# Weight sums moved into the room of the conversion's buffers (three and six of them), the first weight piece converted ahead of the fourth chunk's scores, and the conversion steps dealt out anew

## The chip, the cores and the metric

One core of a Trainium2 chip. The metric is the device time of one execution in microseconds (us); a profile's span is about 2 us shorter. The granted TensorE clock is given where it matters. Names of engines: PE is TensorE's matmul, PEld its weight load, DVE is VectorE, ACT ScalarE, POOL GpSimd, SPq the queue that issues DMAs.

## The reference, cut to what matters

```python
# q, k, v: (8, 8, 576, 64) float32; w1, w2, w3: (512, 768), w_out: (768, 512), all float64
scores = q @ k.T / 8;  ret = scores * decay_mask;  attn = ret @ v       # per batch and head
x = attn.transpose(0, 2, 1, 3).reshape(4608, 512)
h = maximum(maximum(x @ w1, x @ w2), x @ w3)
return (h @ w_out).astype(float32)
```

The weights arrive as float64. The kernel reads them as pairs of 32-bit words and builds float32 values: 24 pieces of 128x512, each by four VectorE steps, three ScalarE steps and one product on GpSimd.

## The kernel before

Attention runs in 36 chunks of 128 tokens, the maxout layer in 9 tiles of 512 tokens. Tile 0 uses plain matrix products and takes place while the weights are being converted; the later tiles use a Strassen-like scheme with sums of weights, which must wait for converted ones. Conversion is a generator; `convert(n)` runs n of its steps, and these calls are strewn between the products, so they fix the order of instructions on VectorE, ScalarE and GpSimd.

```python
wraw = ...tile_pool(name="wraw", bufs=WAHEAD)      # WAHEAD = 4: raw 64-bit pieces
wtmp = ...tile_pool(name="wtmp", bufs=2)           # expo and mant of a piece
...
def convert_all():
    last = None
    for piece in pieces + [None]:
        if piece:                                                       # step a
            nc.vector.tensor_scalar(out=expo[:], in0=high, scalar1=0x7FF00000, ...)        # "mask"
            nc.scalar.activation(mant[:], low, ...)
        yield
        if piece:                                                       # step b
            nc.scalar.activation(expo...)
            nc.vector.tensor_scalar(out=frac[:], in0=high, scalar1=0xFFFFF, ...)
        yield
        if last:                                                        # step c, of the piece before
            nc.vector.scalar_tensor_tensor(out=e[:], in0=h, ..., in1=e[:], ...)            # "sign"
            nc.gpsimd.tensor_tensor(w, m[:], e[:].bitcast(FP32), op=ALU.mult)              # "product"
            load_weights(1)
        if piece: nc.scalar.activation(expo...)
        yield
        if piece:                                                       # step d
            nc.vector.scalar_tensor_tensor(out=mant[:], in0=frac[:], ..., in1=mant[:], ...)# "whole"
        yield
        last = piece and (piece, high, expo, mant)
...
def ffn(t):                                       # tile 0
    for n, (fp, i) in enumerate(units):           # 3 groups fp, 3 weights i
        for fb in (2 * fp, 2 * fp + 1):
            up_plain(t, h, fb, i)                 # 4 matmuls; i == 0: ScalarE copies h,
            convert(7 if i == 0 else 4)           # i > 0: VectorE takes the maximum
        yield                                     # (a step of attention's next chunk comes here)
    convert(4 * len(pieces) + 4)
    ... down(t, h, m) ...                         # 4 x 6 matmuls with w_out
...
    scores(2); scores(3)
    convert(2)
    values(2)
    convert(3); decay_values(4)
    values(3)
    convert(3)
```

Each matmul written here is two instructions of 4-byte data in the trace, so a piece's product of 4 matmuls is 8 instructions.

Of the kernel before, what the change touches and what calls it, by code (L numbers as in the profile page):

```python
# [46 lines left out]
AHEAD = 3  # L47
WAHEAD = 4


@with_exitstack
def kernel(
# [37 lines left out]
    wraw = while_converting.enter_context(tc.tile_pool(name="wraw", bufs=WAHEAD))  # L90
    wtmp = while_converting.enter_context(tc.tile_pool(name="wtmp", bufs=2))
    ps_r = ctx.enter_context(tc.tile_pool(name="ps_r", bufs=4, space=PSUM))
# [175 lines left out]
    def sums_of_outs():  # L268

        while_converting.close()  # L270
        pool = ctx.enter_context(tc.tile_pool(name="late", bufs=1))
        lo, hi = slice(0, DM // 2), slice(DM // 2, DM)
# [84 lines left out]
    def convert_all():  # L357


        last = None  # L360
        for piece in pieces + [None]:
            if piece:
                raw_bits = bits.pop(piece)
                words = raw_bits[:].bitcast(I32).rearrange("p (f two) -> p f two", two=2)
                high = words[:, :, 1]
                low = raw_bits[:].bitcast(U32).rearrange("p (f two) -> p f two", two=2)[:, :, 0]
                expo = wtmp.tile([P, DM], I32, tag="expo", name="expo")
                mant = wtmp.tile([P, DM], FP32, tag="mant", name="mant")
                nc.vector.tensor_scalar(out=expo[:], in0=high, scalar1=0x7FF00000, scalar2=None, op0=ALU.bitwise_and)  # L369
                nc.scalar.activation(mant[:], low, AF.Identity, bias=one[:], scale=2.0 ** -52)  # L370
            yield
            if piece:
                nc.scalar.activation(expo[:].bitcast(FP32), expo[:], AF.Relu, bias=top[:], scale=-8.0)
                frac = wtmp.tile([P, DM], I32, tag="frac", name="frac", bufs=1)
                nc.vector.tensor_scalar(out=frac[:], in0=high, scalar1=0xFFFFF, scalar2=None, op0=ALU.bitwise_and)
            yield
            if last:
                (i, fb), h, e, m = last
                nc.vector.scalar_tensor_tensor(out=e[:], in0=h, scalar=-2 ** 31, in1=e[:],  # L379
                                               op0=ALU.bitwise_and, op1=ALU.bitwise_or)  # L380
                if i == "out":
                    w = w_sb[i, fb] = w_out[:, fb // 2, fb % 2, :]
                else:
                    w = w_sb[i, fb] = const.tile([P, DM], FP32, name=f"w{i}_{fb}")[:]
                nc.gpsimd.tensor_tensor(w, m[:], e[:].bitcast(FP32), op=ALU.mult)  # L385
                load_weights(1)
            if piece:
                nc.scalar.activation(expo[:], expo[:].bitcast(FP32), AF.Relu, bias=inf[:], scale=-1.0)
            yield
            if piece:  # L390
                nc.vector.scalar_tensor_tensor(out=mant[:], in0=frac[:], scalar=2.0 ** -20, in1=mant[:],
                                               op0=ALU.mult, op1=ALU.add)
            yield
            last = piece and (piece, high, expo, mant)

    def weight_sums(n):
        if n >= len(units):
            return
        fp, i = units[n]
        half = [slice(0, DM // 2), slice(DM // 2, DM)]  # L400
        b11, b21 = (w_sb[i, 2 * fp][:, r] for r in half)
        b12, b22 = (w_sb[i, 2 * fp + 1][:, r] for r in half)
        t1, t2, t4 = (const.tile([P, DM // 2], FP32, name=f"T{m}_{i}_{fp}")[:] for m in (1, 2, 4))
        nc.vector.tensor_tensor(t1, b12, b11, op=ALU.subtract)
        nc.vector.tensor_tensor(t2, b22, t1, op=ALU.subtract)
        nc.gpsimd.tensor_tensor(b12, b22, b12, op=ALU.subtract)
        nc.gpsimd.tensor_tensor(t4, b21, t2, op=ALU.subtract)
        wT[fp, i] = {1: b11, 2: b21, 3: b22, 4: t4, 5: t1, 6: t2, 7: b12}
# [3 lines left out]
    def convert(n):  # L412
        for _ in range(n):
            next(converting, None)
# [56 lines left out]
    def down(t, h, m):  # L471
        ps = ps_y.tile([P, DM], FP32, tag="y", name="down")
        for fb in range(NF):
            nc.tensor.matmul(ps[:], lhsT=h[:, fb, m * P:(m + 1) * P], rhs=w_sb["out", fb],  # L474
                             start=(fb == 0), stop=(fb == NF - 1))
        osb = wtmp.tile([P, DM], FP32, tag="mant", name="osb")
        nc.scalar.copy(osb[:], ps[:])
# [12 lines left out]
    def ffn(t):  # L490

        h = hpool.tile([P, NF, NT], FP32, tag="h", name="h")
        for n, (fp, i) in enumerate(units):
            if t == 0:
                for fb in (2 * fp, 2 * fp + 1):
                    up_plain(t, h, fb, i)
                    convert(7 if i == 0 else 4)
            else:
# [9 lines left out]
        if t == 0:  # L508
            convert(4 * len(pieces) + 4)
            for m in range(NT // P):  # L510
# [21 lines left out]
    load(4)  # L532
    load_weights(2)
    decay_values(0)
# [11 lines left out]
    values(1)  # L546
    scores(2)
    scores(3)
    convert(2)
    values(2)  # L550
    convert(3)
    decay_values(4)
    values(3)
    convert(3)
    for t in range(N // NT):
        work = ffn(t)
        for g in range((t + 1) * CPT, (t + 2) * CPT):
            for step in (transposes, scores, values):
                if g < NG:
                    if step is transposes and g + 1 < NG:  # L560
                        load(g + 1)
                    if step is scores and g + 1 < NG:
                        decay_values(g + 1)
                    step(g)
                next(work, None)
# [51 lines left out]
```

## Time and profile before

| what | before |
|---|---|
| median time of the first runs | 848.0 us |
| span of the profile | 845.1 us |
| PE busy | 830.1 us, 98% |
| start of the first up product | 33.40 us |
| start of the first down product | 114.33 us |
| first product of the second tile | 144.76 us |

The table by stretches, cut at these three places, has in each line the stretch, its length, the busy time of each engine with its count of instructions (in the order PE, PEld, DVE, ACT, POOL), the granted clock of TensorE (1.00 is full), the DMA share and GB/s. It is the view to begin with.

```profile
0.00:33.40 33.40, 27.24 (x252) 24.07 (x252) 14.84 (x27) 11.05 (x17) 12.45 (x19) 1.00 0.80 199
33.40:114.30 80.90, 80.34 (x312) 40.93 (x313) 57.01 (x105) 48.75 (x73) 38.16 (x25) 0.98 0.55 161
114.30:144.80 30.50, 27.15 (x99) 13.27 (x98) 15.10 (x21) 5.17 (x9) 13.25 (x11) 0.94 0.22 55
144.80:845.10 700.30, 695.40 (x3977) 594.32 (x3975) 327.46 (x652) 110.07 (x297) 125.93 (x127) 1.00 0.26 54
```

The last stretch has five sixths of the time, and TensorE is busy in all but 5 us of it. What can be won lies in the first three: idle time, and a clock of 0.98 and 0.94, which "busy" does not show.

### The profile page before, as it was taken

The page shows a single profiled execution, that of the slowest core. Times are in us where ns is not written, and L with a number is a line of the kernel's source. Part 1 is how long each engine was busy: PE and PEld are TensorE (multiplying, and loading weights), DVE is VectorE, ACT ScalarE, POOL GpSimd, SP SyncE. Part 2 cuts the span into 40 slices and gives each one's busy share as a digit, 9 for nine tenths or more (in the row PEclk, how much of TensorE's full clock was granted, in tenths as well). Part 3 has the DMA queues.
Part 4 walks back from the last instruction along what each step waited for, and adds up shares of the span by engine and source line. Part 5 has one row for each costly group of instructions (what it writes and reads, how often), then busy time and mean ns, then how long its engine had stood idle before and what let it go on. Part 6 is the DMA issues. An engine that isn't in the chain of part 4 may idle for free.

```text
span 845.1 us, 12652 instructions
## 1 busy us (share of the span) xinstructions
PE 830.1 (98%) x4636; PEld 672.6 (80%) x4636; DVE 414.4 (49%) x803; ACT 175.0 (21%) x395; POOL 189.8 (22%) x182
## 2 busy tenths in 40 slices
PE   9799989999999999999999999999999999999998
PEld 8455445878888888888888888888888888888887
DVE  2577754575445534554454435444345435433341
ACT  3356731111011111111111111111111111111211
POOL 3345544254301211111111121112011202201000
PEclk9999999999999999999999999999999999999999
DMA  9636631333223322333133323332333224201001
GB/s 233 166 125 187 187 69 58 56 56 56 57 53 75 57 55 54 56 62 82 50 56 54 57 77 56 56 56 68 69 54 55 50 62 77 50 14 37 1 1 50
DMA packets 232509, 59.06 MB, mean 70 GB/s; under 512 B 213504, under 2 KB 230912, under 8 KB 232448
## 3 DMA queue, kind: packets, MB, share of 16 engines
q1 hardware_dynamic: 232304, 58.26, 30.7%
q8 instruction: 36, 0.59, 0.3%
q14 instruction: 25, 0.20, 0.1%
q10 hardware_dynamic: 144, 0.00, 0.0%
HBM read 48.76 MB, written 9.44 MB: 69 GB/s over the span
## 4 chain that ended last, share of the span: by engine, by line
PE 86%; DVE 6%; POOL 4%; issue 1%; SPq 1%; DMA 0%; ACT 0%; DVEq 0%; POOLq 0%
PE x L425 28%; PE z L425 14%; PE dx L312 10%; PE y L425 7%; PE dz L312 5%; PE s L183 4%; PE o L213 4%; PE kv L194 4%; PE o L218 4%; POOL w L385 3%; PE dy L312 2%; PE down L474 2%; DVE expo L379 2%; DVE expo L369 1%; SPq L146 1%
## 5 line engine op out<-in xcount | busy, mean ns | idle before, releaser
L425 PE MATMUL x<-S,T 128*128 128x256 f32 x576 | 147.8, 379 | 0.0
L425 PEld LDWEIGHTS x<-S,T 128*128 128x128 f32 x576 | 109.2, 190 | 15.2
L156 POOL TENSOR_TENSOR vd<-vraw,gk 128x512 f32<-128x512 f32 x36 | 38.3, 1064 | 340.6 <-DMA vraw<-in_v_dram 334.5
L425 PE MATMUL x<-S,w 128*128 128x256 f32 x288 | 74.6, 381 | 1.4 <-DVE h L455 1.4
L425 PE MATMUL x<-xT,w 128*128 128x256 f32 x288 | 74.8, 382 | 0.0
L425 PE MATMUL z<-S,w 128*128 128x256 f32 x288 | 73.9, 379 | 0.0
L425 PE MATMUL z<-xT,T 128*128 128x256 f32 x288 | 73.9, 379 | 0.0
L425 PE MATMUL y<-xT,w 128*128 128x256 f32 x288 | 73.9, 379 | 0.0
L430 ACT COPY p<-x 128x256 f32<-128x256 f32 x72 | 26.8, 372 | 220.6 <-PE x L425 217.9
L455 DVE TENSOR_TENSOR tmp<-x,p 128x256 f32<-128x256 f32 x48 | 20.4, 425 | 102.4 <-PE x L425 102.4
L483 PE MATMUL up<-xT,w 128*128 128x512 f32 x144 | 65.8, 609 | 4.8 <-POOL w L385 4.7
L186 DVE TENSOR_TENSOR st<-s,causal 128x512 f32<-128x512 f32 x72 | 46.4, 685 | 48.3 <-PE s L183 48.3
L425 PEld LDWEIGHTS x<-S,w 128*128 128x128 f32 x288 | 49.3, 189 | 15.2 <-DVE h L455 2.4
L425 PEld LDWEIGHTS z<-S,w 128*128 128x128 f32 x288 | 54.7, 190 | 7.4
L425 PEld LDWEIGHTS y<-xT,w 128*128 128x128 f32 x288 | 54.7, 190 | 7.4
L425 PEld LDWEIGHTS z<-xT,T 128*128 128x128 f32 x288 | 54.0, 189 | 8.2
L220 DVE TENSOR_TENSOR xT<-o,gq 128x512 f32<-128x512 f32 x36 | 24.8, 690 | 72.2 <-PE o L218 66.2
L425 PEld LDWEIGHTS x<-xT,w 128*128 128x128 f32 x288 | 51.5, 190 | 6.6 <-issue 0.8
L483 PEld LDWEIGHTS up<-xT,w 128*128 128x128 f32 x144 | 27.0, 194 | 37.3 <-issue 29.8
L295 POOL TENSOR_TENSOR H<-h 128x256 f32<-128x256 f32 x24 | 18.6, 774 | 150.4 <-DVE h L468 150.4
L430 ACT COPY u<-x 128x256 f32<-128x256 f32 x72 | 26.8, 372 | 99.9 <-PE x L425 99.9
L183 PEld LDWEIGHTS s<-qT,kT 64*128 64x128 f32 x576 | 35.7, 191 | 13.6 <-issue 11.1
(92 smaller groups left out, 1203.6 us busy)
## 6 DMA issues: line engine op xcount, KB each, us to landing
bits<-in_moe_w_dram SPq DMA_DIRECT2D x18, 512.0 KB, 3.6
out_dram<-osb SPq DMA_DIRECT2D x36, 256.0 KB, 2.1
kraw<-in_k_dram SPq DMA_DIRECT2D x32, 256.0 KB, 3.0
vraw<-in_v_dram SPq DMA_DIRECT2D x32, 256.0 KB, 3.5
qraw<-in_q_dram SPq DMA_DIRECT2D x448, 16.0 KB, 1.8
kxraw<-in_k_dram SPq DMA_DIRECT2D x448, 16.0 KB, 1.8
bits<-in_moe_w_out_dram SPq DMA_DIRECT2D x6, 512.0 KB, 3.5
qraw<-in_q_dram SPq DMA_DIRECT2D x7, 256.0 KB, 4.4
```

Of the source, the lines that this page charges most:

```text
L156: nc.gpsimd.tensor_tensor(t[:], raws.pop(("v", g))[:], gk[:].unsqueeze(2).to_broadcast([C, H, D]), op=ALU.mult)
L183: nc.tensor.matmul(s[j][:, p, :], lhsT=kT[r, p, :], rhs=qT[r, p, :], start=True, stop=True)
L186: nc.vector.tensor_tensor(st[:, j], s[j][:], masks[start_of(g)][:].unsqueeze(1).to_broadcast([C, NP, C]), op=ALU.mult)
L194: nc.tensor.matmul(kv[:, p, :], lhsT=pair(kr, p)[r:], rhs=pair(vds[g], p)[r:], start=True, stop=True)
L213: nc.tensor.matmul(o[D * j:D * (j + 1), p, :], lhsT=vr[:, 2 * p + j, :], rhs=st[:, j, p, :], start=(p == 0), stop=(old == 0 and p == NP - ...
L218: nc.tensor.matmul(o[:, p, :old], lhsT=sd[:, p, :], rhs=qT[:, p, :old], start=False, stop=(p == NP - 1), skip_group_check=True)
L220: nc.vector.tensor_tensor(xT[t][:, :, i * C:(i + 1) * C], o[:], gq[:], op=ALU.mult)
L312: nc.tensor.matmul(out[:, m, :], lhsT=hS[n](fp)[:, m * P:(m + 1) * P], rhs=late["T"][n][:, fp, :], start=first and m == 0 and fp == 0, sto ...
L385: nc.gpsimd.tensor_tensor(w, m[:], e[:].bitcast(FP32), op=ALU.mult)
L425: nc.tensor.matmul(out[:], lhsT=w[:, d * P:(d + 1) * P], rhs=xS[t][n][:, d, :], start=first and d == 0, stop=d == 1, skip_group_check=True)
L430: nc.scalar.copy(c[:], src[:])
L483: nc.tensor.matmul(ps[:], lhsT=w_sb[i, fb][:, dc * P:(dc + 1) * P], rhs=xT[t][:, dc, :], start=(dc == 0), stop=(dc == NDC - 1))
```

## The change

The intent: conversion should be ahead of TensorE. The sums of weights, 27 tiles of 1 KB per partition, leave the constants for a pool that opens when conversion's buffers are closed; that pays for a third pair of expo and mant and two more raw buffers. The first piece is masked before the fourth chunk's scores and multiplied right after them. The numbers of steps are dealt out anew.

```diff
-WAHEAD = 4
+WAHEAD = 6
-    wtmp = while_converting.enter_context(tc.tile_pool(name="wtmp", bufs=2))
+    wtmp = while_converting.enter_context(tc.tile_pool(name="wtmp", bufs=3))
... (sums: const.tile -> late["pool"].tile; the outputs' osb: wtmp -> opool; load_weights(2) -> (4) before attention)
+        for n, piece in enumerate(pieces):
+            high, expo, mant, frac = yield from masks(bits.pop(piece))   # steps a, b
+            if last:
+                product(*last)                                          # step c
+                yield
+            whole(mant, frac)                                           # step d
             yield
+            last = piece, high, expo, mant
+            if n == 0:
+                product(*last)
+                yield
+                last = None
+        product(*last)
+        yield
...
-                    convert(7 if i == 0 else 4)
+                    convert(4 if i > 0 else 8 if fp == 1 else 6)
...
     scores(2)
+    convert(3)
+    values(2)
+    decay_values(4)
     scores(3)
+    convert(1)
+    transposes(4)
     convert(2)
-    values(2)
-    convert(3)
-    decay_values(4)
     values(3)
-    convert(3)
+    convert(4)
```

More of the change, by code (lines that the diff above doesn't have):

```diff
@@ L268, in sums_of_outs @@
     def sums_of_outs():
-        while_converting.close()
-        pool = ctx.enter_context(tc.tile_pool(name="late", bufs=1))
+        pool = late["pool"]
         lo, hi = slice(0, DM // 2), slice(DM // 2, DM)
@@ L357, in convert_all @@
     def convert_all():
-        last = None
-        for piece in pieces + [None]:
-            if piece:
-                raw_bits = bits.pop(piece)
-                words = raw_bits[:].bitcast(I32).rearrange("p (f two) -> p f two", two=2)
-                high = words[:, :, 1]
-                low = raw_bits[:].bitcast(U32).rearrange("p (f two) -> p f two", two=2)[:, :, 0]
-                expo = wtmp.tile([P, DM], I32, tag="expo", name="expo")
-                mant = wtmp.tile([P, DM], FP32, tag="mant", name="mant")
-                nc.vector.tensor_scalar(out=expo[:], in0=high, scalar1=0x7FF00000, scalar2=None, op0=ALU.bitwise_and)
-                nc.scalar.activation(mant[:], low, AF.Identity, bias=one[:], scale=2.0 ** -52)
-            yield
-            if piece:
-                nc.scalar.activation(expo[:].bitcast(FP32), expo[:], AF.Relu, bias=top[:], scale=-8.0)
-                frac = wtmp.tile([P, DM], I32, tag="frac", name="frac", bufs=1)
-                nc.vector.tensor_scalar(out=frac[:], in0=high, scalar1=0xFFFFF, scalar2=None, op0=ALU.bitwise_and)
-            yield
-            if last:
-                (i, fb), h, e, m = last
-                nc.vector.scalar_tensor_tensor(out=e[:], in0=h, scalar=-2 ** 31, in1=e[:],
-                                               op0=ALU.bitwise_and, op1=ALU.bitwise_or)
-                if i == "out":
-                    w = w_sb[i, fb] = w_out[:, fb // 2, fb % 2, :]
-                else:
-                    w = w_sb[i, fb] = const.tile([P, DM], FP32, name=f"w{i}_{fb}")[:]
-                nc.gpsimd.tensor_tensor(w, m[:], e[:].bitcast(FP32), op=ALU.mult)
-                load_weights(1)
-            if piece:
-                nc.scalar.activation(expo[:], expo[:].bitcast(FP32), AF.Relu, bias=inf[:], scale=-1.0)
-            yield
-            if piece:
-                nc.vector.scalar_tensor_tensor(out=mant[:], in0=frac[:], scalar=2.0 ** -20, in1=mant[:],
-                                               op0=ALU.mult, op1=ALU.add)
-            yield
-            last = piece and (piece, high, expo, mant)
@@ new lines, in masks @@
+        def masks(raw_bits):
+            words = raw_bits[:].bitcast(I32).rearrange("p (f two) -> p f two", two=2)
+            high = words[:, :, 1]
+            low = raw_bits[:].bitcast(U32).rearrange("p (f two) -> p f two", two=2)[:, :, 0]
+            expo = wtmp.tile([P, DM], I32, tag="expo", name="expo")
+            mant = wtmp.tile([P, DM], FP32, tag="mant", name="mant")
+            nc.vector.tensor_scalar(out=expo[:], in0=high, scalar1=0x7FF00000, scalar2=None, op0=ALU.bitwise_and)
+            nc.scalar.activation(mant[:], low, AF.Identity, bias=one[:], scale=2.0 ** -52)
+            yield
+            nc.scalar.activation(expo[:].bitcast(FP32), expo[:], AF.Relu, bias=top[:], scale=-8.0)
+            frac = wtmp.tile([P, DM], I32, tag="frac", name="frac", bufs=1)
+            nc.vector.tensor_scalar(out=frac[:], in0=high, scalar1=0xFFFFF, scalar2=None, op0=ALU.bitwise_and)
+            nc.scalar.activation(expo[:], expo[:].bitcast(FP32), AF.Relu, bias=inf[:], scale=-1.0)
+            yield
+            return high, expo, mant, frac
@@ new lines, in whole, with product @@
+        def whole(mant, frac):
+            nc.vector.scalar_tensor_tensor(out=mant[:], in0=frac[:], scalar=2.0 ** -20, in1=mant[:],
+                                           op0=ALU.mult, op1=ALU.add)
+        def product(piece, high, expo, mant):
+            i, fb = piece
+            nc.vector.scalar_tensor_tensor(out=expo[:], in0=high, scalar=-2 ** 31, in1=expo[:],
+                                           op0=ALU.bitwise_and, op1=ALU.bitwise_or)
+            if i == "out":
+                w = w_sb[piece] = w_out[:, fb // 2, fb % 2, :]
+            else:
+                w = w_sb[piece] = const.tile([P, DM], FP32, name=f"w{i}_{fb}")[:]
+            nc.gpsimd.tensor_tensor(w, mant[:], expo[:].bitcast(FP32), op=ALU.mult)
+            load_weights(1)
@@ L396, in weight_sums @@
+        last = None
+        for n, piece in enumerate(pieces):
[4 more added lines that the diff above has]
+            whole(mant, frac)
+            yield
+            last = piece, high, expo, mant
+            if n == 0:
+                product(*last)
+                yield
+                last = None
+        product(*last)
+        yield
     def weight_sums(n):
@@ L402, in weight_sums @@
         b12, b22 = (w_sb[i, 2 * fp + 1][:, r] for r in half)
-        t1, t2, t4 = (const.tile([P, DM // 2], FP32, name=f"T{m}_{i}_{fp}")[:] for m in (1, 2, 4))
+        t1, t2, t4 = (late["pool"].tile([P, DM // 2], FP32, name=f"T{m}_{i}_{fp}")[:] for m in (1, 2, 4))
         nc.vector.tensor_tensor(t1, b12, b11, op=ALU.subtract)
@@ L475, in down @@
                              start=(fb == 0), stop=(fb == NF - 1))
-        osb = wtmp.tile([P, DM], FP32, tag="mant", name="osb")
+        osb = opool.tile([P, DM], FP32, tag="osb", name="osb")
         nc.scalar.copy(osb[:], ps[:])
@@ L508, in ffn @@
         if t == 0:
-            convert(4 * len(pieces) + 4)
+            convert(4 * len(pieces))
+            while_converting.close()
+            late["pool"] = ctx.enter_context(tc.tile_pool(name="late", bufs=1))
             for m in range(NT // P):
@@ L532 @@
     load(4)
-    load_weights(2)
+    load_weights(4)
     decay_values(0)
@@ L563 @@
                         decay_values(g + 1)
-                    step(g)
+                    if g > CPT or step is not transposes:
+                        step(g)
                 next(work, None)
```

## The prediction

> **What bounds the kernel now.** I read the page first. TensorE leads it, and nothing else is near.
>
> ```profile
> PE 830.1 (98%) x4636; PEld 672.6 (80%) x4636; DVE 414.4 (49%) x803; ACT 175.0 (21%) x395; POOL 189.8 (22%) x182
> ```
>
> 98% of 845.1 us leaves 15.0 us without a matmul, so a change that only moves work can win little more than that. The table by stretches says where it lies: from 200 to 835 us TensorE is busy without a gap (sum 0), and the last 11 us hold 4.4 us of landing output. About 10.6 us are left, all before 200 us. Next the view of waits for TensorE alone:
>
> ```profile
> PE up L483 <- POOL w L385: 4.7, 1, 4.7
> PE down L474 <- POOL w_out L385: 3.4, 2, 2.6
> PE warm L113 <- POOL ident masks.py:199: 1.4, 1, 1.4
> PE x L425 <- DVE h L455: 1.4, 2, 0.7
> PE o L213 <- DVE st L186: 0.4, 2, 0.2
> ```
>
> Two waits carry it, both for converted weights (GpSimd's multiplication ends a piece): one before the first piece of all, one before the last pieces of w_out. Then the timeline of the weight loads, which shows the pitch of the matmuls (the matmul rows merge and their ends are modelled):
>
> ```profile
> 33.40 0.30 PEld L483 LDWEIGHTS up<-xT,w 128*128 128x128 f32 x2 [4.89 <-POOL w L385]
> 34.00 0.33 PEld L483 LDWEIGHTS up<-xT,w 128*128 128x128 f32 x1 [0.30 <-issue]
> 34.86 0.33 PEld L483 LDWEIGHTS up<-xT,w 128*128 128x128 f32 x1 [0.52 <-issue]
> 35.71 0.33 PEld L483 LDWEIGHTS up<-xT,w 128*128 128x128 f32 x1 [0.52 <-issue]
> 36.56 0.33 PEld L483 LDWEIGHTS up<-xT,w 128*128 128x128 f32 x1 [0.52 <-issue]
> 37.35 0.19 PEld L483 LDWEIGHTS up<-xT,w 128*128 128x128 f32 x1 [0.46 <-issue]
> 37.78 0.19 PEld L483 LDWEIGHTS up<-xT,w 128*128 128x128 f32 x1 [0.24 <-issue]
> ...
> 120.54 0.30 PEld L474 LDWEIGHTS down<-w_out,h 128*128 128x128 f32 x2 [3.42 <-POOL w_out L385]
> 122.43 0.37 PEld L474 LDWEIGHTS down<-w_out,h 128*128 128x128 f32 x2 [1.59 <-POOL w_out L385]
> 124.30 1.77 PEld L183 LDWEIGHTS s<-qT,kT 64*128 64x128 f32 x16 [1.50 <-issue]
> ```
>
> The reader is to see that a wait costs more than its own length: after the first, the pitch is 0.85 us, and 0.43 only from 37.35 on. The first two pieces (16 instructions) take 33.40 to 42.16 = 8.76 us where 16 x 0.43 = 6.9 would do: 1.9 us lost on top of 4.7. After the second wait the scores at 124.30 take 1.90 us; elsewhere the same 16 take 1.09.
>
> Last, VectorE's and GpSimd's timelines while they convert:
>
> ```profile
> 69.63 0.70 DVE L391 SCALAR_TENSOR_TENSOR mant<-frac,mant 128x512 f32<-128x512 int32 x1
> 71.49 0.43 DVE L369 TENSOR_SCALAR expo<-bits 128x512 int32<-128x512 int32 x1 [1.16 <-POOL w L385]
> 71.83 0.42 DVE L375 TENSOR_SCALAR frac<-bits 128x512 int32<-128x512 int32 x1
> 72.17 0.69 DVE L379 SCALAR_TENSOR_TENSOR expo<-bits,expo 128x512 int32<-128x512 int32 x1
> 72.77 0.69 DVE L391 SCALAR_TENSOR_TENSOR mant<-frac,mant 128x512 f32<-128x512 int32 x1
> ```
>
> ```profile
> 69.81 1.65 POOL L385 TENSOR_TENSOR w<-mant,expo 128x512 f32<-128x512 f32 x1 [1.49 <-DVE expo L379]
> 72.93 1.66 POOL L385 TENSOR_TENSOR w<-mant,expo 128x512 f32<-128x512 f32 x1 [1.48 <-DVE expo L379]
> ```
>
> One piece costs a period of 72.93 - 69.81 = 3.12 us: 1.97 us of VectorE (71.49 to 73.46), then 1.16 us in which VectorE waits for the product, because with two buffers the mask of a piece needs the buffer that the product two pieces before still reads. With VectorE's maxima (0.6 each), evictions and masks of attention a piece comes every 4 us (24 pieces from 26.5 to 122.4), just TensorE's own pace (3.44 a piece plus attention). So conversion is a second bound of this stage, 4 us behind at its end: the last maximum ran at 117.48, though its matmuls had ended at 113.45.
>
> **What the Trainium skill says.** "SBUF — State Buffer", section "Who interferes with whom": a VectorE instruction with two SBUF inputs, or in a two-port mode, and a GpSimd instruction that reads SBUF exclude each other for the whole instruction. The trace agrees: the product takes 1.65 us behind L391 and 1.26 at 34.83, where VectorE was free; the 0.42-us mask took 1.50 at 26.81 under GpSimd's state product; an eviction from PSUM at 28.23 kept its 0.68 beside a GpSimd product. "TensorE: Matmul & The Clock Gate", Part 1: the clock halves after an idle window of about 3.4 us, free-running, and returns after a busy one. Agrees: half pitch for some 3.5 us after 33.40. The same page, "Architectural detail", has VectorE and ScalarE as strict FIFOs, so program order decides what a late operand holds up.
>
> **The change part by part.**
> (1) Room. The 27 sum tiles of 1 KB leave the constants and go where conversion's buffers stood; that pays for a third pair of expo and mant and six raw buffers. It moves no instruction; the sums start after the last conversion anyway. The outputs of the plain down products get another two-buffer pool: 4 copies, 0.58 us each, 5 us apart: nothing.
> (2) Three buffers remove the 1.16-us buffer wait, but the lock stays. A piece needs 1.97 us of VectorE and 1.26 of GpSimd, and all four VectorE steps exclude GpSimd: 3.23 us if nothing else lies between, no better than 3.12. Only VectorE's work from PSUM (0.6 us a piece or so) can now run in GpSimd's shadow. I book no gain in period, only slack.
> (3) First piece earlier. The order listing puts its masks before the fourth chunk's scores, its sign and product right after; before, they stood behind the second piece's masks and an eviction. Its bits had landed at 19.97 (ScalarE's wait for them ended there), so the masks need not wait. By hand with the trace's durations: second half of chunk 2's masked scores ends 21.7; VectorE takes state, expo 22.2, frac held by GpSimd's state product to 24.0, whole 24.6, eviction 25.2, fourth masked scores 26.4, state 27.0, sign 27.65. GpSimd: state product to 28.9, weight product to 30.5. VectorE's next masks, caught behind these, end about 30.9, and the eviction of chunk 3 stands behind them: 31.5. TensorE, with values(2), scores(3), transposes and values(3) in the new order, ends at 29.0. So the first up product starts at 31.5 (range 30.5 to 32.5) in place of 33.40: 1.9 us won, and an idle of 2.5 us in place of 4.7. Whether the clock drops after 2.5 us depends on the window's phase; I give 30%, so 0.7 x 1.9 = 1.3 us won. Together 3.2.
> (4) Ahead of TensorE. 10 steps instead of 8 run before the first product; the further steps are 6, 8 and 6 per product in place of 7, and the last maximum is followed by one piece's two VectorE steps in place of three. The waits for pieces five, six and eight (0.14, 0.4, 0.3, seen at 53.48, 57.20 and near 65.2) and for the masked scores (0.4) should go: 1.2 us. At the end, counting 3.13 a piece plus maxima and attention from the fp=1 group on, VectorE catches up with TensorE near 84 us and again near 97; the last product of up ends near 109.5, the last maximum 110.1, whole and sign 111.3, GpSimd 112.7. The first down product starts near 110.4 and wants that piece 10 instructions later, 114.7. So both waits go: 124.30 - (114.33 + 12 x 0.43) = 4.8 us and the slow scores' 0.8: 5.6.
> Sum: 3.2 + 1.2 + 5.6 = 10.0 us. All of it lies on TensorE's path, and from there on the kernel is the same and TensorE-bound, so it moves the end one for one. I give back 0.5 us, my own guess, for small new waits near the start, where most of the order changes: 848.0 - 9.5 = 838.5 us.
>
> **The rivals.** (a) The lock holds conversion back: if GpSimd and VectorE interleave badly, the last w_out piece is late again, up to the old 4 us plus slow clock. For it: the period is at the lock's limit already. Against: 2 us of slack by my count. It makes 842 to 844. (b) The early masks hold up attention: VectorE is a FIFO, and the fourth scores' mask and two evictions now stand behind three steps. If these delay TensorE to beyond 32 us and the clock still drops, the first item shrinks to about 1: 841. (c) All goes well, first product at 30.5 with full clock, no give-back: 2.9 + 1.9 + 1.2 + 5.6 = 11.6, so 836.4. (d) The sums' new room makes them wait for released buffers, delaying the second tile: nothing speaks for it, as conversion ends 15 us before the first sum (122.4 against 137.7). (e) Earlier weight loads (six ahead) delay the next k, q, v: they queue behind two loads that wait for signs at 27 and 33 us, but are wanted only from 45 us on; no cost.
>
> **Range and chances.** Most likely 838.5; a to c span 836 to 843, so 835.5 to 843.5 eight times in ten. Faster by over 2% needs under 831, 17 us off, more than all idle there is: 0.01. Slower by over 2% would need a mistake of another kind: 0.01. Within 2%: 0.98.
>
> **What would show it.** First up product at 31.5, not 33.40, and its pitch 0.43 from the start (step 3, clock); masks of expo no longer waiting 1.16 us for GpSimd, yet products still about 3.1 us apart, with stretched mask or sign durations in place of the wait (step 2); no wait for w_out, down starting near 110 and the second tile's first product near 135 in place of 144.76 (step 4); the stretch after it unchanged. I am wrong if TensorE waits in a new place before 40 us, if the last w_out piece comes after 115 us, or if the part after the second tile's start changes by over 1 us.

## The result, and the profile after

The changed kernel took 836.82 us in the median (836.0 to 838.54, 4 runs), the kernel before 848.04 us on the same chip. The ratio of the fast runs is 0.987, 95% interval 0.9849 to 0.989: 1.3% less, within the 2% that counts as the same. Ratios are computed as the mean time of one kernel's fast runs over that of the other's fast runs of the same rounds, so they are not quite the ratios of the medians quoted. The span fell by 10.6 us, from 845.1 to 834.5.

The same table by stretches for the changed kernel, cut at its own three places:

```profile
0.00:31.60 31.60, 27.55 (x252) 24.16 (x253) 16.14 (x26) 11.78 (x18) 12.47 (x19) 1.00 0.93 244
31.60:109.10 77.50, 77.47 (x312) 40.18 (x313) 71.23 (x113) 50.57 (x77) 38.23 (x27) 1.00 0.58 163
109.10:134.00 24.90, 24.90 (x98) 12.59 (x97) 10.76 (x15) 2.62 (x5) 9.98 (x9) 1.00 0.12 41
134.00:834.50 700.50, 695.40 (x3977) 594.37 (x3975) 327.77 (x652) 110.17 (x297) 126.23 (x127) 1.00 0.26 54
```

The last stretch is as long as before (700.5 against 700.3). The first lost 1.8 us, the second 3.4, the third 5.6, and the clock is 1.00 throughout. Where the waits went, from the view of waits for TensorE:

```profile
PE up L493 <- DVE xT L220: 2.3, 1, 2.3
PE x L435 <- DVE h L465: 1.6, 2, 0.8
PE warm L113 <- POOL ident masks.py:199: 1.4, 1, 1.4
PE qt L173 <- DMA qraw<-in_q_dram: 0.3, 1, 0.3
```

Both waits for GpSimd's products are gone; what is left ahead of the first up product is 2.3 us for an eviction by VectorE, which ended at 31.48. (The view of the weight loads names the product `w` instead, but that ended at 30.59.) The weight loads after it:

```profile
31.60 0.30 PEld L493 LDWEIGHTS up<-xT,w 128*128 128x128 f32 x2 [2.47 <-POOL w L387]
32.13 0.19 PEld L493 LDWEIGHTS up<-xT,w 128*128 128x128 f32 x1 [0.24 <-issue]
...
35.13 0.30 PEld L493 LDWEIGHTS up<-xT,w 128*128 128x128 f32 x2 [0.66 <-POOL w L387]
```

The pitch is 0.43 us from the start. Only the second piece's first load, at 35.13, comes 0.42 us late. VectorE and GpSimd while they convert, one view each:

```profile
65.47 0.68 DVE L376 SCALAR_TENSOR_TENSOR mant<-frac,mant 128x512 f32<-128x512 int32 x1
66.07 1.50 DVE L365 TENSOR_SCALAR expo<-bits 128x512 int32<-128x512 int32 x1
67.49 0.41 DVE L370 TENSOR_SCALAR frac<-bits 128x512 int32<-128x512 int32 x1
67.83 0.68 DVE L381 SCALAR_TENSOR_TENSOR expo<-bits,expo 128x512 int32<-128x512 int32 x1
```

```profile
65.63 1.65 POOL L387 TENSOR_TENSOR w<-mant,expo 128x512 f32<-128x512 f32 x1 [1.30 <-DVE expo L381]
68.58 1.66 POOL L387 TENSOR_TENSOR w<-mant,expo 128x512 f32<-128x512 f32 x1 [1.30 <-DVE expo L381]
```

The wait of 1.16 us before the mask has become a mask of 1.50 us in place of 0.43. The period, between pieces with no other VectorE work, went from 3.12 to 68.58 - 65.63 = 2.95 us. VectorE's busy time in the second stretch rose from 57.0 to 71.2 us with nearly the same work: a good part of it is waiting inside instructions.

### The profile page after: what moved, and what is told of

Its sections match the earlier page's. It is cut to its first block, busy times and chain, and to the rows that moved or that the text cites. A ratio compares the mean times of both kernels' runs of the same rounds, so it can differ in the third digit from the quotient of the medians.

```text
span 834.5 us, 12656 instructions
## 1 busy us (share of the span) xinstructions
PE 825.3 (99%) x4636; PEld 671.3 (80%) x4636; DVE 425.9 (51%) x803; ACT 175.1 (21%) x395; POOL 186.9 (22%) x182
## 4 chain that ended last, share of the span: by engine, by line
PE 96%; SPq 1%; DVE 1%; DMA 1%; issue 0%; ACT 0%; POOL 0%; POOLq 0%; DVEq 0%
PE x L435 29%; PE z L435 14%; PE dx L311 10%; PE up L493 7%; PE y L435 7%; PE dz L311 5%; PE s L183 5%; PE o L213 4%; PE o L218 4%; PE kv L194 4%; PE dy L311 2%; PE down L484 2%; SPq L146 1%; DMA qraw<-in_q_dram 1%; PE warm L113 1%; PE kt L173 0%
## 5 line engine op out<-in xcount | busy, mean ns | idle before, releaser
L493 PE MATMUL up<-xT,w 128*128 128x512 f32 x144 | 63.6, 594 | 2.3 <-DVE xT L220 2.3
L454 DVE TENSOR_TENSOR tmp<-y,p 128x256 f32<-128x256 f32 x48 | 20.4, 425 | 51.5 <-PE y L435 51.5
```

What stands on the lines that cost most here:

```text
L454: nc.vector.tensor_tensor(c11, y[:], p1[:], op=ALU.add)
L493: nc.tensor.matmul(ps[:], lhsT=w_sb[i, fb][:, dc * P:(dc + 1) * P], rhs=xT[t][:, dc, :], start=(dc == 0), stop=(dc == NDC - 1))
```

## The experiments

The total alone could not say which part of the change did this. My theory was: the order and the step counts bring the gain, the room brings none. The rival: the third buffer does.

TensorE's first up product starts 1 to 2 us earlier or later from run to run with the first loads (30.5 to 31.7 us in most traces that have the changed kernel's start order, 35.1 in one), so for each experiment I also give the **length of the stage** from that product's start to the second tile's first product, which does not contain these waits; it does contain any half clock after the product's start. Before it is 144.76 - 33.40 = 111.4 us, after 134.02 - 31.63 = 102.4 us.

### Room alone

```diff
 # the kernel before, with
-WAHEAD = 4          / wtmp bufs=2
+WAHEAD = 6          / wtmp bufs=3; sums in the late pool, osb in opool
```

> The kernel before with the room alone: three pairs of expo and mant, six raw buffers, sums and outputs in other pools; order of work as before. Theory (order and step counts bring the gain): the first up product still waits until about 33.4 us and runs at half pitch; the 1.16-us buffer wait of VectorE's mask is replaced by a stretched mask (about 1.5 us under GpSimd's product), period of a piece 2.96 in place of 3.12; the end of conversion comes 1 to 3 us earlier, so 845 to 847 us. Rival (the buffers are the cause): period near 2 us and 840 us or less.

844.18 us (841.61 to 847.04), before 846.63 on this chip; ratio 0.9967 (0.9949 to 0.9985). Stage 108.1 us. VectorE's timeline:

```profile
70.10 1.50 DVE L368 TENSOR_SCALAR expo<-bits 128x512 int32<-128x512 int32 x1
...
73.06 1.50 DVE L368 TENSOR_SCALAR expo<-bits 128x512 int32<-128x512 int32 x1
```

Period 73.06 - 70.10 = 2.96 us, with the stretched mask, as the theory said. The relative gain of some 2.5 us is in its range; the absolute figure is 0.8 us under it, partly because this chip's kernel before is 1.4 us faster than the first. The wait for w_out shrank from 3.4 to 1.7 us. So the room is worth something where conversion is late, but a fifth of the whole.

### Order and counts alone

```diff
 # the changed kernel, with
-WAHEAD = 6          / wtmp bufs=3          / load_weights(4)
+WAHEAD = 4          / wtmp bufs=2          / load_weights(2)   (as before)
```

> The changed kernel with two pairs of expo and mant and four raw buffers again: order and step counts alone. Theory: first up product at 31.6 us, pitch 0.43; conversion's last piece 2 to 3 us later than in the changed kernel (111.7), so no wait or one under 1 us before the last w_out piece: 837 to 838.5 us. Rival (the third buffer is needed): the waits for w_out come back with their slow clock, 841 us or more.

835.51 us (835.15 to 835.74), ratio 0.9867 (0.9855 to 0.988). Stage 132.92 - 30.53 = 102.4 us, the same as the full change. No wait for w_out. So all of the gain is in the order and the counts. I had expected 837 to 838.5: the time is 1.5 us under that, and the allowance for a later last piece (2 to 3 us) was not needed.

### Late start

```diff
 # the changed kernel, with the start of before and no early first product
     scores(2)
-    convert(3); values(2); decay_values(4); scores(3); convert(1)
-    transposes(4); convert(2); values(3); convert(4)
+    scores(3); convert(2); values(2); convert(3); decay_values(4)
+    values(3); convert(5); transposes(4)
-            if n == 0:
+            if False:
```

> The changed kernel with the start in the order of before (fourth scores ahead of all conversion, first product after the second piece's masks), ten steps before the first up product. Theory: the first up product waits until about 33.4 us and runs at half pitch to about 37.3, costing 3.4 us: 840.2 us; the wait for w_out stays away. Rival (the early start is what keeps conversion ahead to the end): w_out waits come back, 844 us or more.

839.96 us (839.73 to 840.09), ratio 0.992 (0.9907 to 0.9933). The first up product waits 4.7 us again and starts at half pitch; no wait for w_out. Against 835.5 of the run before, the early start is worth 4.4 us, while three fifths of the gain ((846.63 - 839.96) / (846.63 - 835.51) = 0.60) remain without it.

### Warm matmuls in the wait

```diff
 # the kernel before, with
     values(3)
     convert(3)
+    transposes(CPT)
+    warm(16)            # 32 instructions of 128x128 in TensorE's idle time
```

> The kernel before with 32 dummy 128x128 matmuls in TensorE's idle time ahead of the first up product, the wait itself untouched. Theory (1.9 us of the first wait's cost is the clock, not the wait): first up product still at 33.4 us, pitch 0.43 from the start, first two pieces in 6.9 us in place of 8.8; 846.1 us. Rival (the slow pitch comes from something else, such as VectorE or DMA traffic): pitch stays 0.85, 848 us.

845.5 us (843.94 to 846.81), ratio 0.9986 (0.9972 to 0.9999). The weight loads:

```profile
33.53 0.30 PEld L483 LDWEIGHTS up<-xT,w 128*128 128x128 f32 x2 [1.28 <-POOL w L385]
34.07 0.19 PEld L483 LDWEIGHTS up<-xT,w 128*128 128x128 f32 x1 [0.24 <-issue]
```

The wait ends at the same time, but the pitch is 0.43 at once: the first two pieces take 40.60 - 33.53 = 7.1 us, not 8.8. So that loss was the clock, as said. In the medians only 1.1 us of it arrives; the wait for w_out is still 2.6 us here, and the runs with a granted clock of 0.995 are the slower ones.

### Once more the changed kernel

> The changed kernel once more, beside its variants on one chip. Theory from the order-only run (which needed neither the third buffer nor six raw ones): the same as order-only, 835 to 837 us. Rival (the room still brings something here): over 1 us faster than order-only's 835.5.

836.17 us (835.38 to 836.97), ratio 0.9871. Stage 102.4 us. The room adds nothing to the order.

### One step fewer

By now it was shown that the order does it, but not which part of the order. Comparing VectorE's rows of the kernel before and of order-only, I saw that the maxima stood in another place. In the kernel before 8 of the 12 (the groups fp=0 and fp=2) come between a piece's masks and its sign, 4 (fp=1) behind `whole`; in the changed kernel all 12 come right behind the sign, that is, just when GpSimd starts its product, and attention's masked scores and evictions with them. A maximum reads one operand from PSUM and one from SBUF. I call this the phase. One step fewer at the start turns it back, so that all 12 stand between masks and sign:

```diff
 # order-only, with
     values(3)
-    convert(4)
+    convert(3)
```

> Order-only (two and four buffers) with 9 in place of 10 steps before the first up product: every maximum and masked score of VectorE then falls between a piece's masks and its sign, as in the kernel before, in place of right behind the sign. Theory (phase: behind the sign these PSUM instructions run while GpSimd multiplies, elsewhere they add 0.6 us each to the period): VectorE is 2 to 4 us behind TensorE at the last maximum, waits for w_out of 1 to 3 us and slow clock come back: 838 to 841 us. Rival (phase does not matter, only how much is done ahead; one step is a quarter of a piece): 835.5 to 836.2 us.

846.07 us (843.76 to 849.84), ratio 0.9992 (0.9974 to 1.001): nearly the whole gain is gone, more than I expected. Stage 147.54 - 35.11 = 112.4 us. (The traced run is the slowest of the six, with a granted clock of 0.994: two waits for a first load, 2.0 us, and matmuls at half speed near 20 us, 2.08 us where 1.16 is usual, are behind its late start at 35.11. The stage length leaves that out.) First order-only, then this run, VectorE near the end of conversion:

```profile
99.78 0.68 DVE L381 SCALAR_TENSOR_TENSOR expo<-bits,expo 128x512 int32<-128x512 int32 x1
100.39 0.67 DVE L498 TENSOR_TENSOR h<-h,up 128x512 f32<-128x512 f32 x1
100.98 1.38 DVE L376 SCALAR_TENSOR_TENSOR mant<-frac,mant 128x512 f32<-128x512 int32 x1
...
104.16 0.67 DVE L498 TENSOR_TENSOR h<-h,up 128x512 f32<-128x512 f32 x1
```

```profile
113.83 0.68 DVE L498 TENSOR_TENSOR h<-h,up 128x512 f32<-128x512 f32 x1
114.43 0.68 DVE L381 SCALAR_TENSOR_TENSOR expo<-bits,expo 128x512 int32<-128x512 int32 x1
115.03 0.68 DVE L376 SCALAR_TENSOR_TENSOR mant<-frac,mant 128x512 f32<-128x512 int32 x1
116.88 0.43 DVE L365 TENSOR_SCALAR expo<-bits 128x512 int32<-128x512 int32 x1 [1.16 <-POOL w_out L387]
...
118.16 0.68 DVE L498 TENSOR_TENSOR h<-h,up 128x512 f32<-128x512 f32 x1
```

In the first the maximum keeps its 0.67 us while GpSimd multiplies (its product runs from 100.54), and the next `whole` waits inside itself to 102.4. From one maximum to the next it is 3.77 us. In the second it is 4.33, because nothing fills the time of the product; both stretches hold one maximum and one eviction besides the four steps. In all traces a maximum takes 0.67 to 0.70 us, beside a product or not, and a product with a maximum right behind its sign 1.26 to 1.29 in 39 of 40 cases (1.71 in one), hardly more than the 1.26 of a product alone. TensorE needs a piece every 3.44 us plus attention, so the first keeps up and the second falls behind. Its waits:

```profile
PE up L493 <- DVE xT L220: 2.5, 1, 2.5
PE s L183 <- ACT qT L175: 2.4, 1, 2.4
PE qt L173 <- DMA qraw<-in_q_dram: 2.0, 2, 1.8
PE down L484 <- POOL w_out L387: 1.8, 2, 1.0
PE o L213 <- DVE st L186: 1.5, 2, 1.3
```

The wait for scores comes from ScalarE, whose timeline ahead of it reads:

```profile
96.72 0.78 ACT L366 ACTIVATE mant<-bits,one 128x512 f32<-128x512 uint32 x1 [1.57 <-POOL w L387]
...
98.78 0.57 ACT L175 COPY kT<-kt 128x512 f32<-128x512 f32 x1
99.24 0.59 ACT L175 COPY qT<-qt 128x512 f32<-128x512 f32 x1
```

Its step on the raw piece waits for a product, since with two buffers `mant` is still being read. Attention's two copies stand behind it in program order, and TensorE's scores wait for them. So a late product does not only delay weights: through GpSimd and ScalarE, which work in program order here, it delays attention. I did not foresee this.

### The old counts

```diff
 # order-only, with
-                    convert(4 if i > 0 else 8 if fp == 1 else 6)
+                    convert(4 if i > 0 else 7)
```

> Order-only with the old step counts, 7 per product of the first weight and 4 elsewhere, in place of 6, 8 and 6. This shifts the phase by two in the groups fp=0 and fp=2 and leaves it in fp=1. Theory: maxima of fp=0 and fp=2 outside GpSimd's shadow, VectorE 2 to 4 us behind near the end, but the last piece comes before the last maximum in program order: 835.5 to 837.5 us, with a small wait before down at most. Rival (the even counts are what keeps conversion ahead): 839 us or more.

839.68 us (838.65 to 840.48), ratio 0.9914 (0.9901 to 0.9927). I expected 835.5 to 837.5, so this is a miss by 2 to 3 us and lies in the range of the rival (839 or more: "the even counts are what keeps conversion ahead"). It is in the direction of the phase: with 7 steps, seven maxima stand between the two masks and five behind the sign. TensorE waits 1.0 us for masked scores and 0.3 for w_out, and stage length is 106.1 us. Part of it is the clock, as the weight loads of the traced run show:

```profile
31.08 0.50 PEld L493 LDWEIGHTS up<-xT,w 128*128 128x128 f32 x2 [2.47 <-POOL w L387]
32.10 0.34 PEld L493 LDWEIGHTS up<-xT,w 128*128 128x128 f32 x1 [0.52 <-issue]
```

The changed kernel shows the same 2.47 us in front of its first load and full pitch after it; here the pitch is half, 0.85 us. So the counts 6, 8, 6 matter, and the clock after a wait of this length can go either way.

### Bad phase, more ahead

If order matters only through "being ahead", three more steps at the start must bring the gain back. If the phase decides, they must not, as 13 steps have the same phase as 9.

```diff
 # order-only, with
     values(3)
-    convert(4)
+    convert(7)
```

> Order-only with 13 steps before the first up product: the bad phase of the phase-back run (maxima between masks and sign), but three quarters of a piece more done ahead than order-only. Theory (phase): 842 to 847 us, as phase-back. Rival (phase-back lost because less was done ahead): 835.5 or less.

843.32 us (842.57 to 845.68), before 847.29 on this chip; ratio 0.9957 (0.9943 to 0.9971). Stage 109.5 us. Three steps more than order-only, and it is 8 us slower; four steps more than the run with one step fewer gain 2.7 us. TensorE waits 2.6 us for masked scores and 1.9 for qT here, and not for w_out: being further ahead removes that wait, but the loss in attention stays.

### The phase, in the kernel before

```diff
 # the kernel before, with
     values(3)
-    convert(3)
+    convert(2)
-                    convert(7 if i == 0 else 4)
+                    convert(4 if i > 0 else 8 if fp == 1 else 6)
```

> The kernel before, start order, buffers and all, with only the counts changed: 7 steps in place of 8 before the first up product (less ahead), and 6, 8 and 6 per product in place of 7. Every maximum then falls right behind a sign. Theory (phase): the first wait and its slow clock stay (33.4 us, 6.6 us lost), the waits for w_out go: 840 to 843 us. Rival (the early start or work done ahead matters): 847 us or more, since it does less ahead.

842.02 us (840.39 to 842.6), ratio 0.9934 (0.992 to 0.9947). Stage 106.8 us. The step fewer brings the maxima behind the sign, and the counts keep them there in all three groups. One step **less** is done ahead, with the old generator, the old room and the late start untouched, and it is 5.3 us faster. TensorE's waits:

```profile
PE up L483 <- POOL w L385: 4.7, 1, 4.7
PE down L474 <- POOL w_out L385: 0.8, 1, 0.8
```

The first wait is as before; that for w_out went from 3.4 to 0.8 us.

### Bad phase, product on VectorE

If the bad phase costs because VectorE's time from PSUM no longer lies beside GpSimd's product, then with no product on GpSimd it must cost nothing, although VectorE gets more work.

```diff
 # the run with one step fewer, with
-                nc.gpsimd.tensor_tensor(w, m[:], ...)
+                nc.vector.tensor_tensor(w, m[:], ...)
```

> The phase-back kernel (two buffers, 9 steps) with all 24 products of conversion on VectorE in place of GpSimd. Theory (the bad phase costs because VectorE cannot use the time of GpSimd's products, which exclude it): a piece takes about 2.6 us of VectorE and no wait in place of 3.12, phase no longer matters, waits for w_out go: 835 to 838 us although VectorE does more. Rival (phase acts through something else, such as ScalarE's order): 843 us or more.

835.93 us (834.78 to 837.79), ratio 0.9867 (0.9854 to 0.9881). Stage 102.3 us. VectorE's timeline:

```profile
57.19 0.69 DVE L387 TENSOR_TENSOR w<-mant,expo 128x512 f32<-128x512 f32 x1
57.80 0.68 DVE L376 SCALAR_TENSOR_TENSOR mant<-frac,mant 128x512 f32<-128x512 int32 x1
58.40 0.42 DVE L365 TENSOR_SCALAR expo<-bits 128x512 int32<-128x512 int32 x1
58.74 0.42 DVE L370 TENSOR_SCALAR frac<-bits 128x512 int32<-128x512 int32 x1
59.07 0.68 DVE L381 SCALAR_TENSOR_TENSOR expo<-bits,expo 128x512 int32<-128x512 int32 x1
59.79 0.69 DVE L387 TENSOR_TENSOR w<-mant,expo 128x512 f32<-128x512 f32 x1
```

Five steps on one engine take 59.79 - 57.19 = 2.60 us, less than four steps and GpSimd's product together (3.12), because the two exclude each other and GpSimd needs 1.26 us alone for what VectorE does in 0.69. The same bad phase, the same counts, and the 10 us are back. This run alone could also mean that any faster conversion suffices; together with the two runs before it, which change nothing in the speed of a step, it fits the phase.

### Bad phase, with the room

```diff
 # the changed kernel, with
     values(3)
-    convert(4)
+    convert(3)
```

> The changed kernel, three and six buffers, with 9 in place of 10 steps: the bad phase with the room. Theory (the third buffer only turns the wait into a stretched mask): 843 to 846 us, at most 2.5 us better than phase-back, as room-only was against before. Rival (the room makes the kernel robust against the phase): 838 us or less.

842.14 us (839.81 to 843.92), ratio 0.9937 (0.9921 to 0.9953). Stage 108.2 us. The same one step less as above, but with three and six buffers: it costs some 6 us, not 10. (In this trace the first up product also starts at half pitch, up to 35.62.) My lower bound was 843, so the room is worth a little more in the bad phase than I thought: 112.4 - 108.2 = 4.2 us of stage length. In the good phase it is worth nothing.

### Eviction first, second piece early

The other runs pointed at the last idle time at the start: VectorE's eviction of chunk 3 stood behind the second piece's masks. Here it comes ahead of them, and the second piece gets its product out of turn as well.

```diff
 # order-only, with
     convert(1); transposes(4)
-    convert(2); values(3); convert(4)
+    values(3); convert(6)
-            if n == 0:
+            if n < 2:
```

> Order-only with the second piece's masks moved behind the last eviction of the attention output, and the second piece's product, like the first's, right behind its own masks. Theory (the remaining 2.3 us of idle ahead of the first up product are that eviction caught behind two masks that GpSimd holds up): first up product 1.3 us earlier, idle about 1 us, no wait for the second piece: 833.7 to 834.5 us. Rival (the first piece's product on GpSimd sets the start anyway): 835.3 us or more.

835.01 us (834.78 to 835.54), before 847.21; ratio 0.9858 (0.9845 to 0.9871). This is the fastest version run. It beats the changed kernel on the same chip by 1.16 us; I had expected 833.7 to 834.5, so it misses the range by 0.5. Against order and counts, on another chip, the intervals of the ratios overlap (0.9845 to 0.9871 and 0.9855 to 0.988), so that it is faster than that run is not shown. The first up product starts at 30.27, after 1.3 us without a weight load:

```profile
30.27 0.30 PEld L493 LDWEIGHTS up<-xT,w 128*128 128x128 f32 x2 [1.34 <-POOL w L387]
...
34.26 0.30 PEld L493 LDWEIGHTS up<-xT,w 128*128 128x128 f32 x2 [1.11 <-POOL w L387]
```

The wait shrank as expected, but the expected "no wait for the second piece" failed: its first load comes 34.26 - 30.27 = 3.99 us after the first piece's, in the changed kernel 35.13 - 31.60 = 3.53. These 0.46 us are also the difference of the stages (102.9 against 102.4), and they can account for the missing 0.5 us. Waits of 0.6 us for q's and k's first loads, which differ from run to run, stand ahead of the start as well.

### All of it in one table

Overlap is the time that VectorE's maxima, masked scores, states and evictions of the conversion stage lay beside one of GpSimd's weight products, added up from the two timelines (of some 16 us of such work). "Ahead" counts the steps called before the first product; "clock" is the mean granted clock of TensorE in the stage.

| kernel | maxima stand | ahead | room | overlap | stage | clock | median |
|---|---|---|---|---|---|---|---|
| before | 8 before sign, 4 behind whole | 8 | 2 / 4 | 4.0 us | 111.4 us | 0.97 | 846.63 to 848.04 |
| room alone | same | 8 | 3 / 6 | 4.7 | 108.1 | 0.98 | 844.18 |
| one step fewer | 12 before sign | 9 | 2 / 4 | 0 | 112.4 | 0.97 | 846.07 |
| bad phase, more ahead | 11 before sign, 1 behind it | 13 | 2 / 4 | 0.5 | 109.5 | 0.98 | 843.32 |
| bad phase, with room | 12 before sign | 9 | 3 / 6 | 2.0 | 108.2 | 0.98 | 842.14 |
| old counts | 7 between masks, 5 behind sign | 10 | 2 / 4 | 4.2 | 106.1 | 0.99 | 839.68 |
| phase alone | 12 behind sign | 7 | 2 / 4 | 10.3 | 106.8 | 0.97 | 842.02 |
| late start | 12 behind sign | 10 | 3 / 6 | 9.7 | 103.7 | 0.99 | 839.96 |
| order and counts | 12 behind sign | 10 | 2 / 4 | 10.0 | 102.4 | 1.00 | 835.51 |
| changed kernel | 12 behind sign | 10 | 3 / 6 | 9.7 | 102.4 | 1.00 | 836.17 |
| eviction first | 12 behind sign | 10 | 2 / 4 | 10.5 | 102.9 | 1.00 | 835.01 |

Every row with the maxima behind the sign has a shorter stage than every row with them before it, whatever the room and however many steps are done ahead. Old counts, with part of the maxima in each place, lies between the rows of its kind: 102.4 us with all behind the sign, 106.1 with five, 112.4 with none. The stages also hold time at half clock: phase alone runs its first products at half pitch from 33.43 to 39.28. As a rough estimate, the stage times its granted clock takes that out, and the kinds stay apart: 102.4 to 103.6 us with all maxima behind the sign, 105.9 to 109.1 in the other rows but old counts (105.1). The run with the product on VectorE is left out, as it has no product on GpSimd. The medians also hold the start: phase alone and late start still have the wait of 4.7 us ahead of the first product.

## Why the prediction was right or wrong, point by point

The time, 838.5 us, was 1.7 us too high and inside the range; "within 2%" was right. The steps are less right than the sum.

**Step 1, room: "nothing".** Right for the changed kernel. Order and counts without the room took 835.51 us against 846.63, with it 836.17 against 847.21, and the stage is 102.4 us in both. But it is not so in general: in the old order the room gives 2.5 us, in the bad phase some 4.

**Step 2, three buffers: "no gain in period, only slack".** The lock came as described, with a mask of 1.50 us in place of a wait of 1.16. The period fell by 0.17 us, to 2.95, which I had as zero: my sum of four VectorE steps and a product, 3.23 us, was 0.28 too much. What failed is the other half of the step. I wrote that VectorE's work from PSUM "can now run in GpSimd's shadow", tied it to the third buffer and booked nothing for it. The shadow is the mechanism, and it needs no third buffer: it needs the maxima behind the sign, which the order does. With two buffers the overlap is 10.0 us, with three 9.7.

**Step 3, first piece earlier: 31.5 us, 70% of full clock, together 3.2.** It came at 31.63, with 2.3 us of wait for xT, the eviction behind the second piece's masks, as worked out, and at full pitch. The start gave 33.40 - 31.63 = 1.8 us. The first two pieces, up to the scores of attention that follow them, took 8.76 us before; the changed kernel takes 38.76 - 31.63 = 7.13, so 1.6 us more, where the prediction counted 1.9: 3.4 in all. (It read the half pitch after 33.40 as some 3.5 us; its own lines have it until 37.35, 3.95 us.) One sign that I had named for being wrong came in small: a new wait before 40 us, the 0.42 us at 35.13. The late start, a run on the same chip as order-only, gives 4.4 us for the same thing. The 30% chance of a clock drop was a fair guess: of six traces with this idle of 2.31 to 2.32 us, two start at half pitch (old counts; bad phase, with room).

**Step 4, "ahead of TensorE".** The result is as stated: no wait for w_out, the second tile's first product at 134.02 (135 was given), and 144.76 - 114.33 = 30.43 us of the end became 134.02 - 109.12 = 24.90, so 5.5 us against 5.6; the small waits, from the end of the first two pieces to the first down product (114.33 - 42.16 = 72.17 us before, 109.12 - 38.76 = 70.36 after), gave 1.8 us against 1.2. The reason given is what failed. I credited ten steps instead of eight and two VectorE steps instead of three after the last maximum. One step fewer than ten, still one more than before, loses nearly all of it; 13 steps in the bad phase lose some 8 us; seven steps in the good phase, in the old kernel, gain 5.3. My count of step 4 came out right because, as I read it now, I took VectorE's durations from the group fp=1 of before, where the maxima stand behind `whole` and lie beside the product: there the products start at 81.25, 84.39, 87.52 and 90.65, so a piece takes 3.13 us with its maximum, while in the group after it a piece with one maximum takes 110.81 - 107.09 = 3.72. The changed kernel has 86.45 - 83.27 = 3.18 with one. The line, "3.13 a piece plus maxima and attention from the fp=1 group on", does not show which durations it used, so this stays a reading; but that the count fitted a phase I had not seen was luck. It had VectorE catch up with TensorE near 84 us and near 97; in the trace the first maximum after 57 us that waits for TensorE is the one at 105.01.

**The give-back of 0.5 us** was not needed. 3.4 + 1.8 + 5.5 = 10.7 us is the gain of the trace.

**Rivals.** (a), the lock holding conversion back, did not come, but I had called for "2 us of slack" against it when it was one step away: at one step fewer, w_out waits 1.8 us, the scores 2.4, and the time is 846. Slack that is counted with the durations of another order is no evidence. (b) came in part, as the 2.3 us for xT, and was in the 31.5 already. (c), 836.4 with no give-back, is what happened in the total, though not with its 30.5 us start. (d) and (e) left no trace in the waits, but for 0.3 us for q at 16.77, which the run with warm matmuls, with the loads of before, has too (0.3).

**What stays open.** How much of the 2.7 us between nine and thirteen steps in the bad phase is being ahead (the wait for w_out, 1.8 us in the one trace, is gone in the other) and how much is scatter (their ranges, 843.76 to 849.84 and 842.57 to 845.68, overlap); by which of its two parts, the third pair or the six raw buffers, the room gives 2 to 4 us in the other phases, and through which wait; and the first loads, whose waits move the start by about 1 us.

## What to carry to other kernels

Where VectorE and GpSimd share a chain of small steps, place VectorE's instructions that read PSUM right behind the one that starts GpSimd's, so that they run during it; one step of shift here moved 10 us with no instruction added. Before buying buffers against a wait, ask what exclusion the wait was hiding: a removed wait may return as a longer instruction. And count idle time of TensorE before a burst twice, once for its length and once for the clock it can cost afterwards.

## What the Trainium skill lacked or had wrong

- "SBUF — State Buffer", section "Who interferes with whom", agrees with the runs: the lock is there. It does not say that the lock can take the place of a buffer wait that is taken away: the wait of 1.16 us became a mask of 1.50 us in place of 0.43, and the period only went from 3.12 to 2.95 us.
- No page says that the place of PSUM-reading VectorE instructions against GpSimd's decides the time: one conversion step of shift cost 10.6 us (835.51 to 846.07 us, each against a before of 847), and 0 against 10.0 us of work lay beside the product.
- No page gives the sum for a short product on GpSimd against VectorE in a chain under this lock: here GpSimd needs 1.26 us alone and 1.65 when it is issued under VectorE's `whole`, VectorE 0.69, so a piece takes 2.60 us with VectorE alone and 3.12 with both (2.95 with three buffers).
- "TensorE: Matmul & The Clock Gate", Part 1, has the clock fall after an idle window of about 3.4 us, and calls the window free-running. Here 2.31 to 2.32 us without a matmul were enough in two traces (old counts; bad phase, with room) and not in four others with the same idle ahead of the same product (the changed kernel's two, order and counts, bad phase with more ahead); what decides between them is not shown. The same page's section "Why this matters for your kernels" allows gaps of up to some 3 us; a gap of 2.31 us is not safe here, and no sure loss either.
